# Sliding-window attention and a rational FFN: another form of the division, and work moved off GpSimd while weights are decoded

## The chip, the cores and the metric

The kernel runs on one core of one Trainium2 chip. The metric is the device time of one execution in microseconds (us). Engines are called as in the profile: PE (TensorE), PEld (its weight loads), ACT (ScalarE), DVE (VectorE), POOL (GpSimd), SP (it issues all DMAs).

## The reference

Attention over a window of 64 positions, 8 batches of 576 positions with 8 heads of 64, then a feed-forward layer whose activation is a ratio of two polynomials:

```python
scores = scale * np.matmul(q, k.transpose(0, 1, 3, 2))          # (8, 8, 576, 576)
mask = (rel >= 0) & (rel < 64)
attn = softmax(np.where(mask, scores, -1e9)); x = (attn @ v)    # reshaped to (4608, 512)

h = x @ w_in                                                    # (4608, 2048)
P = a[0] + a[1] * h + a[2] * h**2 + a[3] * h**3
Q = 1.0 + np.abs(b[0]) * np.abs(h) + np.abs(b[1]) * h**2
g = P / (Q + 1e-06)
out = g @ w_out                                                 # (4608, 512)
```

`w_in` and `w_out` come as float64 and reach the core as pairs of 32-bit words.

## The kernel before

The 4608 tokens are cut into 12 chunks of 384 (`CH`). A chunk has 4 attention units (one for each pair of heads) and 16 steps, one for each 128 columns of `w_in`. Matrix products are made in fp32r with split operands: each of x, `w_in`, `w_out` and the gate g is held as a high part (rounded to fp32r) and a low part (what is left), and three products are added up.

- **decode** turns one 128x512 tile of float64 words into fp32: a DMA into `w_st` (two buffers), five integer or max steps on DVE (L113 to L118) through `w_c` (two buffers), a cast to the high part on ACT (L121), and the low part as a difference (L122) on POOL. There are 32 tiles, 16 of each matrix.
- **unit_scores** makes scores on PE, scales and masks them (L188 or L192, two halves), takes the row maximum (L198), six exponentials with sums on ACT (L201), the reciprocal of the sums (L203, L204), and the normalization of `sm` (L205) on POOL. unit_transpose and unit_av follow, and leave x as `xh` (ACT, L228) and `xl` (DVE, L229).
- **ffn1** makes one step: 12 matmuls into `h` (PSUM, two buffers), then the gate. `ah` = |h|; the numerator is built in `num` by ACT (L245) and two DVE products with h (L246, L247); the denominator without its constant in `u` by two POOL operations (L248, L249). The reciprocal of u + QADD is exp(-ln(.)) on ACT (L251, L252) with one Newton step on DVE (L253, L254); L255 finishes the quotient in `num`, ACT casts it to `gh` (L258), and the difference `gl` (L260) is on POOL for the first 20 gates (`GLN`) and on DVE for the rest. `ah`, `u` and `num` have two buffers each, `gh` and `gl` four (`LAG` + 1).
- **ffn2** multiplies a step's gh and gl with `w_out`, 9 matmuls, three steps (`LAG`) behind ffn1, and adds into three PSUM tiles for the chunk, which ACT copies out at the chunk's end (L294).

The first two chunks are interleaved by halves (`phases`), so that only half of the weights is wanted at first. The table `todo` says at which step a tile is loaded or a unit made: four tiles of `w_in` and chunk 0's units come ahead of the first step, the other 28 tiles at steps 0 to 22, chunk 1's units at steps 0 to 4, chunk 2's from step 21. The program is written in this order, and the framework's scheduler then lays down a fixed order of instructions for each engine; each engine works in order and waits on semaphores.

Of the kernel before, what the change touches and what calls it, by code (L numbers as in the profile page):

```python
# [31 lines left out]
def swa_rational_ffn(ctx: ExitStack, tc: tile.TileContext, qT, kT, v, w_in, w_out, a, b, out):  # L32
    nc = tc.nc
    P = 128
# [66 lines left out]
    def decode(src, hi, lo):  # L101

        w = stage.tile([P, 512, 2], U32, name="w_st", bufs=2)
        if len(src.shape) == 3:
# [8 lines left out]
        nc.vector.tensor_scalar(out=c, in0=high, scalar1=0x7FFFFFFF, scalar2=None, op0=ALU.bitwise_and)  # L113
        nc.vector.tensor_scalar(out=cf, in0=cf, scalar1=2.0 ** -15, scalar2=None, op0=ALU.max)

        nc.vector.tensor_scalar(out=c, in0=c, scalar1=3, scalar2=0x3FFFFFF8, op0=ALU.logical_shift_left, op1=ALU.bitwise_and)
        nc.vector.scalar_tensor_tensor(out=c, in0=low, scalar=29, in1=c, op0=ALU.logical_shift_right, op1=ALU.bitwise_or)  # L117
        nc.vector.scalar_tensor_tensor(out=c, in0=high, scalar=0xC0000000, in1=c, op0=ALU.bitwise_and, op1=ALU.bitwise_or)  # L118
# [2 lines left out]
        nc.scalar.copy(out=hi, in_=cf)  # L121
        nc.gpsimd.tensor_tensor(out=lo, in0=cf, in1=hi.bitcast(F32), op=ALU.subtract)  # L122
# [49 lines left out]
    def unit_scores(c, hp):  # L172
        u = live[c, hp]

        ps = ps_a.tile([P, 2, 512], F32, name="ps_s", bufs=1)
# [8 lines left out]
        sm = att.tile([P, 2, PR * P], F32, name="sm")
        m0 = u["m0"]
        for z in range(2):
            if m0 is None:
                nc.vector.scalar_tensor_tensor(out=sm[:, z, :].rearrange("p (r c) -> p r c", c=P),  # L188
                                               in0=ps[:, z, 0:PR * P].rearrange("p (r c) -> p r c", c=P), scalar=SCALE,
                                               in1=mask[:, 1:2, :].broadcast_to([P, PR, P]), op0=ALU.mult, op1=ALU.min)  # L190
            else:
                nc.vector.scalar_tensor_tensor(out=sm[:, z, :], in0=ps[:, z, 0:PR * P], scalar=SCALE,  # L192
                                               in1=mask[:, m0:m0 + PR, :].rearrange("p r c -> p (r c)"),
                                               op0=ALU.mult, op1=ALU.min)
# [3 lines left out]
        nc.vector.tensor_reduce(out=nmx, in_=sm, axis=AX.X, op=ALU.max, negate=True)  # L198
        sums = att.tile([P, NR], F32, name="sums")
        for j in range(NR):  # L200
            nc.scalar.activation(sm[:, j, :], sm[:, j, :], AF.Exp, bias=nmx[:, j:j + 1], accum_out=sums[:, j:j + 1])  # L201
# [2 lines left out]
        nc.vector.reciprocal(out=rs, in_=sums)  # L204
        nc.gpsimd.tensor_tensor(out=sm, in0=sm, in1=rs.unsqueeze(2).broadcast_to([P, NR, P]), op=ALU.mult)  # L205
# [26 lines left out]
    n_gates = [0]  # L232

    def ffn1(c, i):
        h = ps_h.tile([P, CH], F32, name="h")
        n = 0
        for cc in range(NCC):
            for w, x in ((wi_h, xl), (wi_h, xh), (wi_l, xh)):
                nc.tensor.matmul(h, w[:, cc, i * P:(i + 1) * P], x[c, cc], start=n == 0, stop=n == 3 * NCC - 1)  # L239
# [4 lines left out]
        nc.scalar.activation(ah, h, AF.Abs)  # L244
        nc.scalar.activation(num, h, AF.Identity, scale=a_sb[:, 3:4], bias=a_sb[:, 2:3])  # L245
        nc.vector.tensor_tensor(out=num, in0=num, in1=h, op=ALU.mult)  # L246
        nc.vector.scalar_tensor_tensor(out=num, in0=num, scalar=a_sb[:, 1:2], in1=h, op0=ALU.add, op1=ALU.mult)  # L247
# [1 line left out]
        nc.gpsimd.tensor_tensor(out=u, in0=u, in1=ah, op=ALU.mult)  # L249

        nc.scalar.activation(ah, u, AF.Ln, bias=QADD)  # L251
        nc.scalar.activation(ah, ah, AF.Exp, scale=-1.0)  # L252
        nc.vector.scalar_tensor_tensor(out=u, in0=u, scalar=QADD, in1=ah, op0=ALU.add, op1=ALU.mult)  # L253
# [1 line left out]
        nc.vector.scalar_tensor_tensor(out=num, in0=num, scalar=a_sb[:, 0:1], in1=u, op0=ALU.add, op1=ALU.mult)  # L255
        gh = gp.tile([P, CH], F32R, name="gh")
        gl = gp.tile([P, CH], F32R, name="gl")
        nc.scalar.copy(out=gh, in_=num)  # L258
# [1 line left out]
        (nc.gpsimd if n_gates[0] <= GLN else nc.vector).tensor_tensor(out=gl, in0=num, in1=gh.bitcast(F32), op=ALU.subtract)  # L260
# [128 lines left out]
```

## Time and profile before

| | us |
|---|---|
| runs of the kernel before | 1063.88, 1064.74, 1066.21 (median 1064.74) |
| the profiled execution | 1063.77 |
| its span, first to last instruction | 1062.0 |
| busy: PE / DVE / ACT / POOL | 963.7 / 917.7 / 674.3 / 525.0 |
| mean granted TensorE clock | 0.966 |

Times in the profile count from the span's start. In a row of the timeline the first number is the start, the second the duration, then engine, line and operation, the tile written and the tiles read, the shape, how many instructions are merged (x2), and in brackets how long the engine was idle before and what ended that. In a table of windows each engine's busy time stands with its number of instructions, then the granted clock, the DMA engines' share and GB/s. In a list of waits stand the total in us, the number of waits and the longest.

The costliest groups outside PE have, over the whole span: L249 on POOL 204.5 us in 192 instructions, L248 on POOL 164.6 in 192, L260 on DVE 154.0 in 172, L245 on ACT 128.5 in 192, L258 on ACT 96.7 in 192.

### The profile page before, as it was taken

How to read it: one execution, taken by the hardware profiler on the slowest of the kernel's cores; microseconds unless marked ns; L12 is line 12 of the kernel's file. 1: busy time of each engine (PE TensorE's matmuls, PEld its weight loads, DVE VectorE, ACT ScalarE, POOL GpSimd, SP SyncE). 2: the span in 40 equal slices, each digit the busy share in tenths (PEclk: the TensorE clock that was granted, in tenths of full speed). 3: DMA queues.
4: the chain of work that ended last, by engine and by line, in shares of the span. 5: the costliest groups of instructions: out<-in, count | busy, mean ns of one | idle time of the engine just before them, and what ended most of it. 6: DMA issues, size and time to landing. Idle time of an engine off the chain costs nothing.

```text
span 1062.0 us, 18218 instructions
## 1 busy us (share of the span) xinstructions
PE 963.7 (91%) x6624; PEld 846.0 (80%) x6624; DVE 917.7 (86%) x1583; ACT 674.3 (63%) x1702; POOL 525.0 (49%) x511
## 2 busy tenths in 40 slices
PE   2558667899999999999999999999999999999997
PEld 2446555778888888888888888888888888888996
DVE  6999989988888898898888888888888888888885
ACT  3454445467666766766766766766666667667654
POOL 5356658864454445435435535534444444454432
PEclk9778779899999999999999999999999999999999
DMA  5543343102121121110211211210211211200000
GB/s 183 173 152 93 107 130 110 35 1 73 48 66 30 59 58 32 63 61 28 70 45 29 69 48 33 92 31 28 85 29 30 88 30 32 93 16 1 31 2 30
DMA packets 68538, 64.10 MB, mean 60 GB/s; under 512 B 4448, under 2 KB 61792, under 8 KB 68448
## 3 DMA queue, kind: packets, MB, share of 16 engines
q1 hardware_dynamic: 68448, 62.93, 19.0%
q8 instruction: 52, 0.85, 0.3%
q14 instruction: 38, 0.31, 0.1%
HBM read 53.48 MB, written 9.44 MB: 59 GB/s over the span
## 4 chain that ended last, share of the span: by engine, by line
DVE 36%; ACT 20%; POOL 19%; PE 17%; issue 5%; DMA 3%; POOLq 0%; SPq 0%; DVEq 0%; ACTq 0%
PE o L280 8%; ACT sm L201 8%; POOL u L248 7%; PE h L239 7%; DVE u L253 7%; POOL u L249 6%; POOL sm L205 4%; DVE u L254 4%; DVE nmx L198 4%; DVE num L255 2%; ACT ah L251 2%; DVE w_c L117 2%; DVE gl L260 2%; ACT ah L252 2%; DVE w_c L118 2%
## 5 line engine op out<-in xcount | busy, mean ns | idle before, releaser
L239 PE MATMUL h<-xl,wi_h 128*128 128x384 f32 x768 | 269.4, 351 | 30.3 <-DVE num L247 22.3
L248 POOL TENSOR_SCALAR u<-ah,b_sb 128x384 f32<-128x384 f32 x192 | 164.6, 860 | 262.8 <-ACT ah L244 199.6
L239 PE MATMUL h<-xh,wi_h 128*128 128x384 f32 x768 | 264.3, 344 | 0.0
L239 PE MATMUL h<-xh,wi_l 128*128 128x384 f32 x768 | 263.5, 343 | 0.0
L280 PE MATMUL o<-wo_h,gl 128*128 128x512 f32 x576 | 236.8, 411 | 25.4 <-DVE gl L260 14.4
L280 PE MATMUL o<-wo_h,gh 128*128 128x512 f32 x576 | 228.6, 397 | 0.0
L280 PE MATMUL o<-wo_l,gh 128*128 128x512 f32 x576 | 228.0, 396 | 0.0
L249 POOL TENSOR_TENSOR u<-u,ah 128x384 f32<-128x384 f32 x192 | 204.5, 1071 | 9.8
L239 PEld LDWEIGHTS h<-xl,wi_h 128*128 128x128 f32 x768 | 148.2, 193 | 40.1 <-DVE num L247 26.1
L205 POOL TENSOR_TENSOR sm<-sm,rs 128x768 f32<-128x768 f32 x48 | 81.4, 1696 | 195.8 <-DVE rs L204 195.8
L201 ACT ACTIVATE sm<-sm,nmx 128x128 f32<-128x128 f32 x288 | 111.9, 390 | 102.7 <-DVE nmx L198 102.4
L260 DVE TENSOR_TENSOR gl<-num,gh 128x384 fp32r<-128x384 f32 x172 | 154.0, 899 | 13.0 <-ACT gh L258 10.0
L245 ACT ACTIVATE num<-h,a_sb 128x384 f32<-128x384 f32 x192 | 128.5, 670 | 45.7 <-DVE gl L260 35.8
L280 PEld LDWEIGHTS o<-wo_h,gl 128*128 128x128 f32 x576 | 109.6, 190 | 58.9 <-DVE gl L260 19.2
L239 PEld LDWEIGHTS h<-xh,wi_h 128*128 128x128 f32 x768 | 148.5, 193 | 4.7
L253 DVE SCALAR_TENSOR_TENSOR u<-u,ah 128x384 f32<-128x384 f32 x192 | 116.7, 608 | 40.9 <-ACT ah L252 39.2
L251 ACT ACTIVATE ah<-u 128x384 f32<-128x384 f32 x192 | 100.4, 523 | 80.2 <-POOL u L249 79.3
L239 PEld LDWEIGHTS h<-xh,wi_l 128*128 128x128 f32 x768 | 148.3, 193 | 0.0
L280 PEld LDWEIGHTS o<-wo_h,gh 128*128 128x128 f32 x576 | 109.7, 190 | 25.2
L258 ACT CAST gh<-num 128x384 fp32r<-128x384 f32 x192 | 96.7, 508 | 47.5 <-DVE num L255 47.4
L280 PEld LDWEIGHTS o<-wo_l,gh 128*128 128x128 f32 x576 | 109.9, 191 | 18.7
L255 DVE SCALAR_TENSOR_TENSOR num<-num,a_sb,u 128x384 f32<-128x384 f32 x192 | 121.1, 636 | 2.9
(45 smaller groups left out, 1274.1 us busy)
## 6 DMA issues: line engine op xcount, KB each, us to landing
out<-ob SPq DMA_DIRECT2D x33, 256.0 KB, 2.0
w_st<-w_in SPq DMA_DIRECT2D x16, 512.0 KB, 3.7
w_st<-w_out SPq DMA_DIRECT2D x16, 512.0 KB, 3.6
q<-qT SPq DMA_DIRECT2D x32, 192.0 KB, 3.4
vt<-v SPq DMA_DIRECT2D x16, 384.0 KB, 3.4
vt<-v SPq DMA_DIRECT2D x16, 320.0 KB, 3.3
kt<-kT SPq DMA_DIRECT2D x16, 224.0 KB, 3.5
kt<-kT SPq DMA_DIRECT2D x16, 192.0 KB, 3.5
```

The costliest lines, as they stand in the source:

```text
L201: nc.scalar.activation(sm[:, j, :], sm[:, j, :], AF.Exp, bias=nmx[:, j:j + 1], accum_out=sums[:, j:j + 1])
L205: nc.gpsimd.tensor_tensor(out=sm, in0=sm, in1=rs.unsqueeze(2).broadcast_to([P, NR, P]), op=ALU.mult)
L239: nc.tensor.matmul(h, w[:, cc, i * P:(i + 1) * P], x[c, cc], start=n == 0, stop=n == 3 * NCC - 1)
L245: nc.scalar.activation(num, h, AF.Identity, scale=a_sb[:, 3:4], bias=a_sb[:, 2:3])
L248: nc.gpsimd.tensor_scalar(out=u, in0=ah, scalar1=b_sb[:, 1:2], scalar2=b_sb[:, 0:1], op0=ALU.mult, op1=ALU.add)
L249: nc.gpsimd.tensor_tensor(out=u, in0=u, in1=ah, op=ALU.mult)
L251: nc.scalar.activation(ah, u, AF.Ln, bias=QADD)
L253: nc.vector.scalar_tensor_tensor(out=u, in0=u, scalar=QADD, in1=ah, op0=ALU.add, op1=ALU.mult)
L255: nc.vector.scalar_tensor_tensor(out=num, in0=num, scalar=a_sb[:, 0:1], in1=u, op0=ALU.add, op1=ALU.mult)
L258: nc.scalar.copy(out=gh, in_=num)
L260: (nc.gpsimd if n_gates[0] <= GLN else nc.vector).tensor_tensor(out=gl, in0=num, in1=gh.bitcast(F32), op=ALU.subtract)
L280: nc.tensor.matmul(acc[c][t], g[:, ts], w[:, i, :], start=first and n == 0, stop=last and n == 2)
```

## The change

Four things change.

1. In decode, the absolute value of the high word is made by ACT (a floating-point Abs of the word) and no longer by DVE, and the low part's difference goes from POOL to DVE.
2. The normalization of `sm` is made by DVE for the units of chunks 0 and 1 (8 of 48).
3. In the gate, the step b1 * ah + b0 goes from POOL to ACT, for all steps. The product u * ah is made by DVE for the first 28 gates (`DEC`) and stays on POOL for the others.
4. The division: with r = exp(-ln(Q)), gh is written at once as (num + a0) * r, rounded to fp32r; u becomes Q * gh; num becomes (num + a0) - u, the remainder; gl = num * r, the low part. So the Newton step and ACT's cast are gone, DVE still has four steps after Exp, and `ah` (which holds r) is read until the last of them.

```diff
-GLN = 20
+DEC = 28
...
-        nc.vector.tensor_scalar(out=c, in0=high, scalar1=0x7FFFFFFF, scalar2=None, op0=ALU.bitwise_and)
+        nc.scalar.activation(cf, w.bitcast(F32)[:, :, 1], AF.Abs)
...
-        nc.gpsimd.tensor_tensor(out=lo, in0=cf, in1=hi.bitcast(F32), op=ALU.subtract)
+        nc.vector.tensor_tensor(out=lo, in0=cf, in1=hi.bitcast(F32), op=ALU.subtract)
...
-        nc.gpsimd.tensor_tensor(out=sm, in0=sm, in1=rs.unsqueeze(2).broadcast_to([P, NR, P]), op=ALU.mult)
+        (nc.vector if c < 2 else nc.gpsimd).tensor_tensor(out=sm, in0=sm, in1=rs.unsqueeze(2).broadcast_to([P, NR, P]), op=ALU.mult)
...
+        gh = gp.tile([P, CH], F32R, name="gh")
+        gl = gp.tile([P, CH], F32R, name="gl")
         nc.scalar.activation(ah, h, AF.Abs)
         nc.scalar.activation(num, h, AF.Identity, scale=a_sb[:, 3:4], bias=a_sb[:, 2:3])
+        nc.scalar.activation(u, ah, AF.Identity, scale=b_sb[:, 1:2], bias=b_sb[:, 0:1])
         nc.vector.tensor_tensor(out=num, in0=num, in1=h, op=ALU.mult)
         nc.vector.scalar_tensor_tensor(out=num, in0=num, scalar=a_sb[:, 1:2], in1=h, op0=ALU.add, op1=ALU.mult)
-        nc.gpsimd.tensor_scalar(out=u, in0=ah, scalar1=b_sb[:, 1:2], scalar2=b_sb[:, 0:1], op0=ALU.mult, op1=ALU.add)
-        nc.gpsimd.tensor_tensor(out=u, in0=u, in1=ah, op=ALU.mult)
+        n_gates[0] += 1
+        (nc.vector if n_gates[0] <= DEC else nc.gpsimd).tensor_tensor(out=u, in0=u, in1=ah, op=ALU.mult)
 
         nc.scalar.activation(ah, u, AF.Ln, bias=QADD)
         nc.scalar.activation(ah, ah, AF.Exp, scale=-1.0)
-        nc.vector.scalar_tensor_tensor(out=u, in0=u, scalar=QADD, in1=ah, op0=ALU.add, op1=ALU.mult)
-        nc.vector.scalar_tensor_tensor(out=u, in0=u, scalar=2.0, in1=ah, op0=ALU.subtract, op1=ALU.mult, reverse0=True)
-        nc.vector.scalar_tensor_tensor(out=num, in0=num, scalar=a_sb[:, 0:1], in1=u, op0=ALU.add, op1=ALU.mult)
-        nc.scalar.copy(out=gh, in_=num)
-        n_gates[0] += 1
-        (nc.gpsimd if n_gates[0] <= GLN else nc.vector).tensor_tensor(out=gl, in0=num, in1=gh.bitcast(F32), op=ALU.subtract)
+        nc.vector.scalar_tensor_tensor(out=gh, in0=num, scalar=a_sb[:, 0:1], in1=ah, op0=ALU.add, op1=ALU.mult)
+        nc.vector.scalar_tensor_tensor(out=u, in0=u, scalar=QADD, in1=gh.bitcast(F32), op0=ALU.add, op1=ALU.mult)
+        nc.vector.scalar_tensor_tensor(out=num, in0=num, scalar=a_sb[:, 0:1], in1=u, op0=ALU.add, op1=ALU.subtract)
+        nc.vector.tensor_tensor(out=gl, in0=num, in1=ah, op=ALU.mult)
```

The new kernel's lines of the gate are L246 to L248 (ACT: Abs, num, u), L249 and L250 (DVE: the products with h), L252 (u * ah), L255 and L256 (Ln, Exp), L257 to L260 (gh, u, num, gl).

The scheduler lays the engines' orders anew. DVE in the ramp, around the second pair of gates, before (`w_c` and `w_st` are the tile in decoding, L229 is an attention unit's):

```order
L113 TENSOR_SCALAR w_c<-w_st 128x512
L114 TENSOR_SCALAR w_c<-w_c 128x512
L229 TENSOR_TENSOR xl_651<-ps_x,xh_650 128x384
L116 TENSOR_SCALAR w_c<-w_c 128x512
L117 SCALAR_TENSOR_TENSOR w_c<-w_st,w_c 128x512
L253 SCALAR_TENSOR_TENSOR u<-u,ah 128x384
L118 SCALAR_TENSOR_TENSOR w_c<-w_st,w_c 128x512
L254 SCALAR_TENSOR_TENSOR u<-u,ah 128x384
L246 TENSOR_TENSOR num<-num,h 128x384
L247 SCALAR_TENSOR_TENSOR num<-num,a_sb,h 128x384
```

The same place of DVE's new order:

```order
L116 TENSOR_SCALAR w_c<-w_c 128x512
L249 TENSOR_TENSOR num<-num,h 128x384
L117 SCALAR_TENSOR_TENSOR w_c<-w_st,w_c 128x512
L252 TENSOR_TENSOR u<-u,ah 128x384
L250 SCALAR_TENSOR_TENSOR num<-num,a_sb,h 128x384
L117 SCALAR_TENSOR_TENSOR w_c<-w_st,w_c 128x512
L252 TENSOR_TENSOR u<-u,ah 128x384
L250 SCALAR_TENSOR_TENSOR num<-num,a_sb,h 128x384
L118 SCALAR_TENSOR_TENSOR w_c<-w_st,w_c 128x512 x2
L257 SCALAR_TENSOR_TENSOR gh<-num,a_sb,ah 128x384
```

Two tiles and two gates now advance in turn, with the products u * ah (L252) between them; L122, the low part, stands a few rows further on.

ACT in the long stage, one pair of steps with an attention unit, before. The number behind a tile's name tells the two steps of the pair apart:

```order
L258 CAST gh_5072<-num_5060 128x384
L244 ACTIVATE ah_5173<-h_5160 128x384
L258 CAST gh_5112<-num_5100 128x384
L245 ACTIVATE num_5175<-h_5160,a_sb_90 128x384
L244 ACTIVATE ah_5239<-h_5226 128x384
L245 ACTIVATE num_5241<-h_5226,a_sb_90 128x384
L251 ACTIVATE ah_5173<-u_5174 128x384
L228 CAST xh3_4992<-ps_x_4979 128x384
L252 ACTIVATE ah_5173<-ah_5173 128x384
L251 ACTIVATE ah_5239<-u_5240 128x384
L252 ACTIVATE ah_5239<-ah_5239 128x384
L201 ACTIVATE sm_5135,sums_5140<-sm_5135,nmx_5138 128x128 x6
```

The same place of ACT's new order:

```order
L246 ACTIVATE ah_5095<-h_5082 128x384
L247 ACTIVATE num_5097<-h_5082,a_sb_90 128x384
L248 ACTIVATE u_5096<-ah_5095,b_sb_92 128x384
L246 ACTIVATE ah_5160<-h_5147 128x384
L247 ACTIVATE num_5162<-h_5147,a_sb_90 128x384
L248 ACTIVATE u_5161<-ah_5160,b_sb_92 128x384
L255 ACTIVATE ah_5095<-u_5096 128x384
L228 CAST xh3_4917<-ps_x_4904 128x384
L256 ACTIVATE ah_5095<-ah_5095 128x384
L255 ACTIVATE ah_5160<-u_5161 128x384
L256 ACTIVATE ah_5160<-ah_5160 128x384
L201 ACTIVATE sm_5057,sums_5062<-sm_5057,nmx_5060 128x128 x6
```

Before, the gh casts of a pair stand behind the six exponentials and among the next pair's first steps; now nothing of a pair is left on ACT behind its last Exp, and each step has three operations at its start.

DVE at the same place, before, the end of a pair with a unit:

```order
L198 TENSOR_REDUCE nmx_5138<-sm_5135 128x6
L255 SCALAR_TENSOR_TENSOR num_5175<-num_5175,a_sb_90,u_5174 128x384
L254 SCALAR_TENSOR_TENSOR u_5240<-u_5240,ah_5239 128x384
L255 SCALAR_TENSOR_TENSOR num_5241<-num_5241,a_sb_90,u_5240 128x384
L203 TENSOR_SCALAR sums_5140<-sums_5140 128x6
L204 RECIPROCAL rs_5147<-sums_5140 128x6
L260 TENSOR_TENSOR gl_5188<-num_5175,gh_5187 128x384
L260 TENSOR_TENSOR gl_5254<-num_5241,gh_5253 128x384
```

And now:

```order
L257 SCALAR_TENSOR_TENSOR gh_4664<-num_4663,a_sb_90,ah_4661 128x384
L257 SCALAR_TENSOR_TENSOR gh_4729<-num_4728,a_sb_90,ah_4726 128x384
L198 TENSOR_REDUCE nmx_4626<-sm_4623 128x6
L258 SCALAR_TENSOR_TENSOR u_4662<-u_4662,gh_4664 128x384
L258 SCALAR_TENSOR_TENSOR u_4727<-u_4727,gh_4729 128x384
L259 SCALAR_TENSOR_TENSOR num_4663<-num_4663,a_sb_90,u_4662 128x384
L259 SCALAR_TENSOR_TENSOR num_4728<-num_4728,a_sb_90,u_4727 128x384
L260 TENSOR_TENSOR gl_4665<-num_4663,ah_4661 128x384
L260 TENSOR_TENSOR gl_4730<-num_4728,ah_4726 128x384
L203 TENSOR_SCALAR sums_4628<-sums_4628 128x6
L204 RECIPROCAL rs_4635<-sums_4628 128x6
```

The two gl stood behind the unit's sums (L203, L204), which need the exponentials; now they stand ahead of them.

More of the change, by code (lines that the diff above doesn't have):

```diff
@@ L243, in ffn1 @@
         num = tmp.tile([P, CH], F32, name="num")
+        gh = gp.tile([P, CH], F32R, name="gh")
+        gl = gp.tile([P, CH], F32R, name="gl")
         nc.scalar.activation(ah, h, AF.Abs)
         nc.scalar.activation(num, h, AF.Identity, scale=a_sb[:, 3:4], bias=a_sb[:, 2:3])
+        nc.scalar.activation(u, ah, AF.Identity, scale=b_sb[:, 1:2], bias=b_sb[:, 0:1])
         nc.vector.tensor_tensor(out=num, in0=num, in1=h, op=ALU.mult)
         nc.vector.scalar_tensor_tensor(out=num, in0=num, scalar=a_sb[:, 1:2], in1=h, op0=ALU.add, op1=ALU.mult)
-        nc.gpsimd.tensor_scalar(out=u, in0=ah, scalar1=b_sb[:, 1:2], scalar2=b_sb[:, 0:1], op0=ALU.mult, op1=ALU.add)
-        nc.gpsimd.tensor_tensor(out=u, in0=u, in1=ah, op=ALU.mult)
+        n_gates[0] += 1
+        (nc.vector if n_gates[0] <= DEC else nc.gpsimd).tensor_tensor(out=u, in0=u, in1=ah, op=ALU.mult)
         nc.scalar.activation(ah, u, AF.Ln, bias=QADD)
         nc.scalar.activation(ah, ah, AF.Exp, scale=-1.0)
-        nc.vector.scalar_tensor_tensor(out=u, in0=u, scalar=QADD, in1=ah, op0=ALU.add, op1=ALU.mult)
-        nc.vector.scalar_tensor_tensor(out=u, in0=u, scalar=2.0, in1=ah, op0=ALU.subtract, op1=ALU.mult, reverse0=True)
[L255 to L258, printed above, removed]
-        n_gates[0] += 1
-        (nc.gpsimd if n_gates[0] <= GLN else nc.vector).tensor_tensor(out=gl, in0=num, in1=gh.bitcast(F32), op=ALU.subtract)
+        nc.vector.scalar_tensor_tensor(out=gh, in0=num, scalar=a_sb[:, 0:1], in1=ah, op0=ALU.add, op1=ALU.mult)
+        nc.vector.scalar_tensor_tensor(out=u, in0=u, scalar=QADD, in1=gh.bitcast(F32), op0=ALU.add, op1=ALU.mult)
+        nc.vector.scalar_tensor_tensor(out=num, in0=num, scalar=a_sb[:, 0:1], in1=u, op0=ALU.add, op1=ALU.subtract)
+        nc.vector.tensor_tensor(out=gl, in0=num, in1=ah, op=ALU.mult)
         gs[c, i] = gh, gl
```

## Prediction

> **What bounds the kernel now.** I read the page first, then the busy time by stage, then who ended the waits of PE in the long stage.
>
> ```profile
> PE   2558667899999999999999999999999999999997
> DVE  6999989988888898898888888888888888888885
> POOL 5356658864454445435435535534444444454432
> ```
>
> Each digit is 26.5 us. The kernel has two stages. In the first eight slices DVE is full and PE is not; in the rest PE is full. The busy times say it in us:
>
> ```profile
> 0.00:207.00 207.00, 128.82 (x880) 107.00 (x881) 189.06 (x299) 96.04 (x257) 129.53 (x118) 0.83 0.40 124
> 266.00:1040.00 774.00, 762.03 (x5329) 677.65 (x5330) 665.62 (x1182) 530.01 (x1334) 359.46 (x358) 1.00 0.15 45
> ```
>
> The columns are PE, PEld, DVE, ACT, POOL, then the granted clock. Up to 207 us, about where the last weight tile is decoded, DVE works 189 of 207 us and PE waits. From 266 to 1040 us PE works 762 of 774 us at full clock. Its 12 us of idle time there have one cause:
>
> ```profile
> PE o L280 <- DVE gl L260: 12.2, 10, 1.6
> ```
>
> Ten waits, one for each 16-step chunk, for the low part gl of a gate. So there are two places to win: the ramp, paced by DVE, and these ten waits. Everything else after 266 us is matmul work that the change does not touch.
>
> **Why DVE takes so long in the ramp.** Two stretches of DVE and what POOL did in the second:
>
> ```profile
> 9.00 0.43 DVE L116 TENSOR_SCALAR w_c<-w_c 128x512 uint32<-128x512 uint32 x1
> 9.34 1.02 DVE L192 SCALAR_TENSOR_TENSOR sm<-ps_s,mask 128x384 f32<-128x384 f32 x2
> 10.27 0.68 DVE L117 SCALAR_TENSOR_TENSOR w_c<-w_st,w_c 128x512 uint32<-128x512 uint32 x1
> 10.87 0.94 DVE L198 TENSOR_REDUCE nmx<-sm 128x6 f32<-128x768 f32 x1
> 11.73 0.68 DVE L118 SCALAR_TENSOR_TENSOR w_c<-w_st,w_c 128x512 uint32<-128x512 uint32 x1
> 12.33 0.42 DVE L113 TENSOR_SCALAR w_c<-w_st 128x512 uint32<-128x512 uint32 x1
> ...
> 17.40 1.57 DVE L114 TENSOR_SCALAR w_c<-w_c 128x512 f32<-128x512 f32 x1
> 19.47 1.64 DVE L117 SCALAR_TENSOR_TENSOR w_c<-w_st,w_c 128x512 uint32<-128x512 uint32 x1
> ```
>
> ```profile
> 17.14 1.55 POOL L205 TENSOR_TENSOR sm<-sm,rs 128x768 f32<-128x768 f32 x1 [0.73 <-DVE rs L204]
> 19.18 1.38 POOL L122 TENSOR_TENSOR wi_l<-w_c,wi_h 128x512 fp32r<-128x512 f32 x1 [0.49 <-ACT wi_h L121]
> ```
>
> The columns are start and duration in us. The L114 at 17.40 lies under the POOL multiply of 17.14 to 18.69 and takes 1.57 us where its kind takes 0.42; the L117 at 19.47 lies under the POOL subtraction and takes 1.64 instead of 0.68. DVE's decode steps stop while POOL works in SBUF. The price of an operation without that is its distance to the next start: 0.34 us for a one-input 128x512 step (9.00 to 9.34), 0.60 for a two-input one (10.27 to 10.87), 0.93 for both mask steps of a unit, 0.86 for the reduction. The gate's own prices:
>
> ```profile
> 87.18 0.55 DVE L246 TENSOR_TENSOR num<-num,h 128x384 f32<-128x384 f32 x1
> 87.64 0.61 DVE L255 SCALAR_TENSOR_TENSOR num<-num,a_sb,u 128x384 f32<-128x384 f32 x1
> 88.17 0.42 DVE L114 TENSOR_SCALAR w_c<-w_c 128x512 f32<-128x512 f32 x1
> 88.51 0.61 DVE L247 SCALAR_TENSOR_TENSOR num<-num,a_sb,h 128x384 f32<-128x384 f32 x1
> 89.03 1.14 DVE L116 TENSOR_SCALAR w_c<-w_c 128x512 uint32<-128x512 uint32 x1
> 90.09 0.55 DVE L253 SCALAR_TENSOR_TENSOR u<-u,ah 128x384 f32<-128x384 f32 x1
> 90.56 0.41 DVE L113 TENSOR_SCALAR w_c<-w_st 128x512 uint32<-128x512 uint32 x1
> ```
>
> 0.46 for a product, 0.53 with a coefficient from a_sb, 0.47 for L253.
>
> **The ramp after the change.** I count DVE's list of the new order up to the last decoded tile: 32 decodes, 11 attention units, 20 gate fronts (two products with h), 20 products u*ah, and 18 to 20 of each of the four closing steps.
> - Decode: two one-input steps (L113 has gone to ACT) and three two-input ones (the subtraction has come from POOL; 0.60, priced as the equally large L117): 2 x 0.34 + 3 x 0.60 = 2.48 us, x32 = 79.4.
> - Units: 0.93 + 0.86 + about 0.7 for the small ones and xl = 2.5, x11 = 27; the normalization that eight of them bring from POOL, 768 elements like the reduction, 0.87, x8 = 7.
> - Gates: 0.46 + 0.53 + 0.47 (the new product) = 1.46, x20 = 29; closing steps 0.53 + 0.47 + 0.53 + 0.47 = 2.0, some x18.5 = 37.
>
> Together 179 us. Before, the list up to the last tile costs 135 us by the same prices (32 x 2.22 for decodes, 10 units, 16 gates), and DVE was busy 189: some 54 us are contention. So the change brings DVE about 36 us of POOL's work and takes nearly all the contention away.
>
> To this come the start, 8.1 us until the first tile lands (first DVE step, 8.08) and 0.6 for ACT's new Abs ahead of it (priced as the casts of a tile), and the time DVE waits within the ramp: 207 - 189 - 8 = 10 us before. Now decoding goes from ACT to DVE to ACT to DVE, so I take more, 17. Bounds: 4 (the order interleaves two tiles and two gates, so little is left open) and 30 (three times today's). The list ends at 179 + 9 + 17 = 205, between 192 and 218. The kernel before is as far, 18 closed gates, here:
>
> ```profile
> 0.00:221.30 221.30, 0.00 (x0) 23.18 (x18) 0.84 0.38 118
> ...
> 219.93 1.31 POOL L260 TENSOR_TENSOR gl<-num,gh 128x384 fp32r<-128x384 f32 x1
> ```
>
> The first is L260 alone: 18 by 221.3. From there PE is dense in both, so the ramp's gain is 221 - 205 = 16, bounds 3 and 29. I take 15, for the units of the third chunk, whose multiply POOL still does at the end of the ramp. ACT has 96 us in 207 and gains 32 Abs of about 0.6 and one exchange of a gh cast for an affine step: some 23 more, no bound. PE's 129 us are covered too.
>
> **A rule against it.** The spacing of DVE's rows carries the sum: 0.46 between starts where the duration is 0.55. The Trainium skill, VectorE: DVE Perf Modes, section "The DRAIN you can't avoid", says that after each DVE operation the next does not start until the pipe is empty. By that every operation costs its duration; with some 365 operations and 0.08 us each the list would be 29 us longer. The rows above disagree with it in that form (87.18 + 0.55 ends behind the start at 87.64).
>
> **The long stage after the change.** gl no longer waits for ACT's gh cast; ACT has an affine step instead (L248), and POOL only the product. But all temporaries have two buffers, and ah now lives until gl, so a pair of steps cannot begin before the pair ahead has closed. That loop must be shorter than PE's work. Prices and PE's pace:
>
> ```profile
> 546.53 0.49 ACT L244 ACTIVATE ah<-h 128x384 f32<-128x384 f32 x1 [0.69 <-PE h L239]
> 546.92 0.67 ACT L245 ACTIVATE num<-h,a_sb 128x384 f32<-128x384 f32 x1
> 547.48 0.51 ACT L258 CAST gh<-num 128x384 fp32r<-128x384 f32 x1
> ...
> 551.21 0.52 ACT L251 ACTIVATE ah<-u 128x384 f32<-128x384 f32 x1
> 551.75 0.53 ACT L252 ACTIVATE ah<-ah 128x384 f32<-128x384 f32 x1
> 555.04 0.40 ACT L201 ACTIVATE sm<-sm,nmx 128x128 f32<-128x128 f32 x1 [2.76 <-DVE nmx L198]
> ...
> 555.44 0.39 ACT L201 ACTIVATE sm<-sm,nmx 128x128 f32<-128x128 f32 x1
> ```
>
> ```profile
> 547.98 1.01 POOL L249 TENSOR_TENSOR u<-u,ah 128x384 f32<-128x384 f32 x1
> ...
> 558.07 1.72 POOL L205 TENSOR_TENSOR sm<-sm,rs 128x768 f32<-128x768 f32 x1 [7.04 <-DVE rs L204]
> ```
>
> ```profile
> 539.31 4.41 PE o L280 x18
> ...
> 617.82 4.41 PE o L280 x18
> ```
>
> A chunk takes 78.5 us (539.31 to 617.82); without its wait of 1.2 PE needs 77.3, or 19.3 for four steps and a unit. The loop, walked by the new order from the first Abs, with 0.1 for a hand-over (an estimate from the rows' gaps):
> - Pair without a unit: ACT needs 2 x (0.39 + 0.56 + 0.56) = 3.0 for Abs, num and the affine step (unknown; between L252's 0.53 and L245's 0.67, I take the latter, since both read two coefficients). POOL's second product ends at 4.2, the second Ln and Exp at 5.3, the second gh starts at 5.4; then num, u and gl of the first step: its gl ends at 7.5, and the next Abs starts at 7.6.
> - Pair with a unit: on DVE from 3.9 on xl 0.47, masks 0.93, gh twice 1.06, reduction 0.86, u twice 0.94, num twice 1.06, gl 0.55: 9.8. ACT's six exponentials of 0.39 run from 7.3 to 9.7 beside it. POOL's normalization (1.72) then delays the next product by 0.9 and that pair by 0.5.
>
> 7.6 + 9.8 + 0.5 = 17.9 against 19.3: PE stays the bound with 1.4 us to spare, and gl comes without the six exponentials in front of its cast. So I take all 12 us of waits as gone; bounds 0 and 12.
>
> **Sum.** Span 1062.0 - 15 - 12 = 1035.0; the execution's own time is 1063.77, so 1.8 more: 1036.8. That execution lies 1 us under the median of 1064.74. I forecast 1037.
>
> **Rivals.**
> 1. The loop of pairs becomes the bound. For it speaks that ACT already waits for gl:
> ```profile
> ACT num L245 <- DVE gl L260: 35.8, 67, 1.3
> ```
> Against it, the walk. It decides from 20.0 us per four steps on: the stage has 774 / 19.6 = 39.5 groups, each now 19.6 with the waits, and 0.4 x 39.5 eats the ramp's 15. At 20.5 it would be 1064 - 15 + 0.9 x 39.5 = 1084, slower. Chance 0.10.
> 2. The ramp does not shorten: ACT, which works in order, waits for tiles and lets DVE wait. DVE would need 32 us of waits in place of 17, beyond my upper bound. 1064 - 12 = 1052. Chance 0.14.
> 3. The ten waits stay, because gl is late for another reason (the three copies of o at a chunk's end, on ACT): 1064 - 15 = 1049. Chance 0.14.
> 4. Both 2 and 3; within 0.2% of before, 1064. Chance 0.05.
> 5. DVE's operations cost their durations: the ramp 29 - 15 = 14 longer, the waits gone: 1066, at the edge of slower. Chance 0.03. This is the skill's rule above.
>
> The forecast itself, 1024 (bounds 29 and 12) to 1049, has 0.52; still more gain 0.02.
>
> **Range and chances.** 0.2% (2 us) is about what a measurement can tell. Faster: 0.52 + 0.02 + 0.14 + 0.14 = 0.82. Same 0.05. Slower 0.10 + 0.03 = 0.13. The range 1021 to 1058 holds the forecast's cases and rivals 2 and 3, and leaves out rivals 1, 4 and 5.
>
> **What would show it.** Decode steps on DVE at 0.42 and 0.68 throughout; the last tile decoded before 207 us; DVE busy about 180 us up to there; no PE wait for gl between 266 and 1040, PE busy above 770 of 774 there. Wrong, if ACT's first Abs of a pair waits for gl while PE waits for h, if DVE's idle time in the ramp is over 30 us, or if DVE's two-input steps stay at 1 us and more.

## The result and the profile after

| | before | after |
|---|---|---|
| median (lowest to highest), us | 1065.47 (1063.88 to 1066.47) | 1023.91 (1023.07 to 1025.14) |
| span of the profiled execution | 1062.0 | 1023.3 |
| 18th low part gl done at | 221.2 | 191.7 |
| last tile decoded at | 209.6 | 200.6 |
| from the 18th gl to the end | 840.8 | 831.6 |

The ratio is 0.9612 (0.9595 to 0.9629). The span is 38.7 us shorter: 29.5 up to the 18th closed gate and 9.2 behind it.

The page after, busy tenths in 40 slices, now 25.6 us each:

```profile
PE   2677876899999999999999999999999999999997
DVE  5999999998878878878878878878888888888785
POOL 2000010002322322322322322322322322322221
```

POOL is nearly empty in the first nine slices. DVE is as full there as before, so it is still the busiest engine of the ramp, but it comes through sooner. PE is full from the ninth slice on.

The windows of the kernel after (PE, PEld, DVE, ACT, POOL, clock, DMA share, GB/s):

```profile
0.00:191.70 191.70, 127.86 (x932) 105.41 (x933) 175.92 (x351) 120.27 (x307) 14.10 (x30) 0.90 0.45 136
...
192.00:207.00 15.00, 14.23 (x63) 12.08 (x62) 14.33 (x28) 11.21 (x23) 0.00 (x0) 0.89 0.01 1
...
0.00:200.70 200.70, 136.86 (x969) 113.26 (x970) 184.38 (x367) 127.04 (x319) 14.10 (x30) 0.90 0.43 130
...
266.00:1000.00 734.00, 734.00 (x5162) 655.80 (x5161) 596.18 (x1140) 542.46 (x1293) 207.58 (x190) 1.00 0.15 46
```

The same milestone before:

```profile
0.00:221.20 221.20, 141.55 (x951) 117.71 (x951) 200.50 (x317) 104.47 (x282) 138.77 (x126) 0.84 0.38 118
```

To the 18th gl DVE now issues 351 instructions in 175.9 us; before it was 317 in 200.5. So it does 34 more in 24.6 us less. By the prediction's prices this list is some 145 us before and 173 after; the busy time lies 56 us above the one and 3 us above the other.

In the long stage PE works 734.00 of 734.00 us, and no wait of PE is left between 266 and 1000 us. (Behind 1000 us there is one of 2.0 us for gl; before there was one of 2.2.)

The 18th gl is not quite the same point in both kernels: in the kernel after, PE has 19 matmuls fewer behind it there (932 and 951), and the low parts of two tiles are still to be made. In the 15 us behind it PE makes 63 matmuls, so 19 are 4.5 us of work. This makes the ramp worth 29.5 - 4.5 = 25 us and the rest 9.2 + 4.5 = 13.7. A count of PE's starts in the traces says the same: the 1300th matmul starts at 249.6 us, before at 274.5. Of the 13.7 us, 12.2 are waits for gl that are gone; no run separates the other 1.5.

The decode steps on DVE, by lines, before (up to 207 us) and after (up to 192 us); the second number after the bar is the mean in ns:

```profile
L118 DVE SCALAR_TENSOR_TENSOR w_c<-w_st,w_c 128x512 uint32<-128x512 uint32 x32 | 33.0, 1035 | 0.1
L117 DVE SCALAR_TENSOR_TENSOR w_c<-w_st,w_c 128x512 uint32<-128x512 uint32 x32 | 30.6, 959 | 0.3
L114 DVE TENSOR_SCALAR w_c<-w_c 128x512 f32<-128x512 f32 x32 | 20.8, 648 | 0.3
L116 DVE TENSOR_SCALAR w_c<-w_c 128x512 uint32<-128x512 uint32 x32 | 19.9, 621 | 0.3
```

```profile
L118 DVE SCALAR_TENSOR_TENSOR w_c<-w_st,w_c 128x512 uint32<-128x512 uint32 x31 | 21.1, 684 | 0.1
L117 DVE SCALAR_TENSOR_TENSOR w_c<-w_st,w_c 128x512 uint32<-128x512 uint32 x31 | 21.1, 684 | 0.1
L114 DVE TENSOR_SCALAR w_c<-w_c 128x512 f32<-128x512 f32 x31 | 14.5, 468 | 12.8 <-ACT w_c L113 12.8
L116 DVE TENSOR_SCALAR w_c<-w_c 128x512 uint32<-128x512 uint32 x31 | 13.0, 419 | 0.1
```

The same four steps are 28 to 34% shorter. What DVE waited for in the first 192 us of the kernel after (us in total, times, longest):

```profile
DVE w_c L114 <- ACT w_c L113: 12.8, 8, 8.4
DVE sums L203 <- ACT sm L201: 1.1, 3, 0.6
DVE sm L188 <- PE ps_s L182: 0.7, 1, 0.7
DVE wi_l L122 <- ACT wi_h L121: 0.3, 1, 0.3
DVE xl L229 <- ACT xh L228: 0.2, 1, 0.2
```

The longest, 8.4, is the start of the program, until the first tile has landed and ACT has made its Abs. Without it 6.7 us are left.

ACT in the long stage (266 to 1000 us), its waits for h and gl, after and before:

```profile
ACT ah L246 <- PE h L239: 75.9, 83, 3.8
...
ACT ah L246 <- DVE gl L260: 2.5, 2, 2.1
```

```profile
ACT num L245 <- DVE gl L260: 34.9, 63, 1.3
...
ACT ah L244 <- PE h L239: 12.8, 19, 0.9
```

Before, the head of a pair waited mostly for the low part of the pair ahead. Now it waits for PE's h, 83 times, and for gl twice: there it is PE that is waited for. The chain that ended last says the same, before and then after:

```profile
DVE 36%; ACT 20%; POOL 19%; PE 17%; issue 5%; DMA 3%; POOLq 0%; SPq 0%; DVEq 0%; ACTq 0%
```

```profile
PE 81%; DVE 11%; ACT 3%; DMA 3%; issue 1%; POOL 0%; SPq 0%; POOLq 0%; ACTq 0%; DVEq 0%
```

### The profile page after: what moved, and what is told of

The parts are those of the page before. It is cut to its first block, busy times and chain, and to the rows that moved or that the text cites. A ratio compares the mean times of both kernels' runs of the same rounds, so it can differ in the third digit from the quotient of the medians.

```text
span 1023.3 us, 18244 instructions
## 1 busy us (share of the span) xinstructions
PE 953.1 (93%) x6624; PEld 840.4 (82%) x6624; DVE 850.3 (83%) x1639; ACT 725.8 (71%) x1734; POOL 233.7 (23%) x231
## 4 chain that ended last, share of the span: by engine, by line
PE 81%; DVE 11%; ACT 3%; DMA 3%; issue 1%; POOL 0%; SPq 0%; POOLq 0%; ACTq 0%; DVEq 0%
PE o L280 37%; PE h L239 35%; PE ps_x L223 3%; PE ps_s L182 3%; PE ps_s L212 3%; DMA w_st<-w_in 1%; DVE w_c L117 1%; DMA w_st<-w_out 1%; ACT sm L201 1%; DVE w_c L118 1%; DVE num L259 1%; DVE gh L257 1%; DVE u L258 1%; DVE num L249 1%; DVE num L250 1%
## 5 line engine op out<-in xcount | busy, mean ns | idle before, releaser
L239 PE MATMUL h<-xl,wi_h 128*128 128x384 f32 x768 | 264.9, 345 | 14.8 <-DVE num L250 8.6
L239 PE MATMUL h<-xh,wi_l 128*128 128x384 f32 x768 | 259.7, 338 | 0.0
L280 PE MATMUL o<-wo_h,gl 128*128 128x512 f32 x576 | 238.1, 413 | 22.3 <-DVE gl L260 22.3
L252 POOL TENSOR_TENSOR u<-u,ah 128x384 f32<-128x384 f32 x164 | 166.7, 1017 | 317.3 <-ACT u L248 278.7
L249 DVE TENSOR_TENSOR num<-num,h 128x384 f32<-128x384 f32 x192 | 106.1, 553 | 108.9 <-ACT num L247 108.7
L246 ACT ACTIVATE ah<-h 128x384 f32<-128x384 f32 x192 | 94.3, 491 | 108.1 <-PE h L239 83.3
L205 POOL TENSOR_TENSOR sm<-sm,rs 128x768 f32<-128x768 f32 x40 | 61.7, 1541 | 457.9 <-DVE rs L204 352.3
L280 PEld LDWEIGHTS o<-wo_h,gl 128*128 128x128 f32 x576 | 111.3, 193 | 51.3 <-DVE gl L260 24.6
L248 ACT ACTIVATE u<-ah,b_sb 128x384 f32<-128x384 f32 x192 | 135.4, 706 | 0.0
L257 DVE SCALAR_TENSOR_TENSOR gh<-num,a_sb,ah 128x384 fp32r<-128x384 f32 x192 | 114.8, 615 | 17.6 <-ACT ah L256 16.9
L250 DVE SCALAR_TENSOR_TENSOR num<-num,a_sb,h 128x384 f32<-128x384 f32 x192 | 117.9, 614 | 5.9
L259 DVE SCALAR_TENSOR_TENSOR num<-num,a_sb,u 128x384 f32<-128x384 f32 x192 | 115.8, 620 | 0.8
```

Of the source, the lines that this page charges most:

```text
L205: (nc.vector if c < 2 else nc.gpsimd).tensor_tensor(out=sm, in0=sm, in1=rs.unsqueeze(2).broadcast_to([P, NR, P]), op=ALU.mult)
L248: nc.scalar.activation(u, ah, AF.Identity, scale=b_sb[:, 1:2], bias=b_sb[:, 0:1])
L252: (nc.vector if n_gates[0] <= DEC else nc.gpsimd).tensor_tensor(out=u, in0=u, in1=ah, op=ALU.mult)
L257: nc.vector.scalar_tensor_tensor(out=gh, in0=num, scalar=a_sb[:, 0:1], in1=ah, op0=ALU.add, op1=ALU.mult)
L280: nc.tensor.matmul(acc[c][t], g[:, ts], w[:, i, :], start=first and n == 0, stop=last and n == 2)
```

## Experiments

The theory: the ramp's gain is contention taken from DVE's operations, the long stage's gain is the new gate. The rivals are in each expectation. The last four columns are of the profiled execution, in us; "it" is the 18th gl. The kernel before had medians of 1065.5 to 1066.0 beside these runs.

| run | median us | ratio to before (95%) | 18th gl at | from there on | DVE busy to it | POOL busy to it |
|---|---|---|---|---|---|---|
| after | 1023.91 | 0.9612 (0.9595 to 0.9629) | 191.7 | 831.6 | 175.9 | 14.1 |
| e1_gate_only | 1041.11 | 0.9765 (0.9749 to 0.9781) | 215.5 | 824.5 | 198.9 | 92.6 |
| e2_offload_only | 1048.35 | 0.9826 (0.9810 to 0.9841) | 200.2 | 846.2 | 182.9 | 12.1 |
| e3_pool_reads | 1087.46 | 1.0202 (1.0187 to 1.0217) | 248.1 | 837.0 | 237.5 | 137.0 |
| e4_pool_writes | 1039.91 | 0.9745 (0.9728 to 0.9763) | 202.0 | 836.2 | 188.0 | 139.4 |
| e5_lo_pool | 1036.26 | 0.9722 (0.9708 to 0.9737) | 206.2 | 828.6 | 189.8 | 59.9 |
| e6_dec0 | 1023.24 | 0.9601 (0.9585 to 0.9617) | 195.3 | 825.8 | 178.6 | 35.4 |
| e7_sm_pool | 1030.20 | 0.9664 (0.9649 to 0.9678) | 199.4 | 826.9 | 180.8 | 28.1 |
| e8_abs_dve | 1036.74 | 0.9732 (0.9716 to 0.9749) | 205.4 | 828.6 | 188.9 | 16.0 |
| e9_affine_act | 1058.21 | 0.9930 (0.9916 to 0.9945) | 212.3 | 845.1 | 195.3 | 115.4 |
| e10_skip_low | 1014.23 | 0.9523 (0.9507 to 0.9539) | 184.0 | 827.3 | 161.8 | 12.1 |
| e11_sm_act | 1025.01 | 0.9623 (0.9608 to 0.9637) | 195.9 | 829.2 | 175.9 | 12.4 |
| e12_sm_act_skip_low | 1016.68 | 0.9541 (0.9526 to 0.9555) | 187.4 | 828.3 | 157.8 | 11.9 |

### The two halves of the change

**e1_gate_only** is the kernel after with decode, the normalizations and the product u * ah (on POOL) as before:

```diff
-DEC = 28
+DEC = 0
-        nc.scalar.activation(cf, w.bitcast(F32)[:, :, 1], AF.Abs)
+        nc.vector.tensor_scalar(out=c, in0=high, scalar1=0x7FFFFFFF, scalar2=None, op0=ALU.bitwise_and)
-        nc.vector.tensor_tensor(out=lo, in0=cf, in1=hi.bitcast(F32), op=ALU.subtract)
+        nc.gpsimd.tensor_tensor(out=lo, in0=cf, in1=hi.bitcast(F32), op=ALU.subtract)
-        (nc.vector if c < 2 else nc.gpsimd).tensor_tensor(out=sm, in0=sm, in1=rs.unsqueeze(2).broadcast_to([P, NR, P]), op=ALU.mult)
+        nc.gpsimd.tensor_tensor(out=sm, in0=sm, in1=rs.unsqueeze(2).broadcast_to([P, NR, P]), op=ALU.mult)
```

> The new gate alone: the division by remainder and the affine step on ACT for all steps, while the decode (its Abs on DVE, its low part on POOL), the normalization of sm and the product u*ah stay where they were before. Theory A (POOL's reads of SBUF stall DVE in the ramp, and the gl wait of the long stage is one of order on ACT): the ten waits of PE for gl go (12 us); in the ramp POOL loses the affine step (22 us) and the 20 gl (21 us) of its 130 us, so a third of the 54 us of contention, 18, and DVE gains 16 x 0.47 = 7.5 us: 11 less. Span 1062 - 23 = 1039, time near 1041. Theory B (the ramp is paced by hops between engines, and POOL's company costs DVE nothing): the gate has one hop fewer, the ramp stays within 3 us, time near 1052.

**e2_offload_only** is the complement: the old division and cast, and POOL empty in the ramp.

```diff
-        nc.scalar.activation(u, ah, AF.Identity, scale=b_sb[:, 1:2], bias=b_sb[:, 0:1])
-        (nc.vector if n_gates[0] <= DEC else nc.gpsimd).tensor_tensor(out=u, in0=u, in1=ah, op=ALU.mult)
+        eng = nc.vector if n_gates[0] <= DEC else nc.gpsimd
+        eng.tensor_scalar(out=u, in0=ah, scalar1=b_sb[:, 1:2], scalar2=b_sb[:, 0:1], op0=ALU.mult, op1=ALU.add)
+        eng.tensor_tensor(out=u, in0=u, in1=ah, op=ALU.mult)
...
+        nc.scalar.copy(out=gh, in_=num)
+        nc.vector.tensor_tensor(out=gl, in0=num, in1=gh.bitcast(F32), op=ALU.subtract)
```

> The old division (Newton step, gh cast on ACT, gl as a difference, always on DVE), with everything else of the change: Abs on ACT, the low part and the first 8 normalizations on DVE, and both steps of u on DVE for the first 28 gates, on POOL after. Theory A: DVE's list in the ramp is that of the changed kernel plus 20 one-input steps of about 0.3 us, 6 us, so the ramp is some 20 to 24 us shorter than before; the ten gl waits stay, 12 us. Time near 1042. Theory B: DVE has some 45 us more work in the ramp and no relief, time 1065 or more.

PE's waits between 266 and 1000 us, all that are listed, in e1_gate_only and then in e2_offload_only:

```profile
PE o L280 <- DVE gl L260: 0.5, 1, 0.5
```

```profile
PE o L281 <- DVE gl L261: 12.2, 9, 1.5
```

The new gate alone takes the ten waits away but for 0.5 us, and the empty POOL alone leaves them as they were. The ramp goes mostly the other way: the 18th gl comes 6 us sooner than before with the gate alone (215.5) and 21 us sooner with the offload alone (200.2). So the waits go with the gate, most of the ramp's gain goes with the offload, and the spans add up: 22.0 + 15.6 = 37.6 of 38.7.

e1_gate_only came out at its expected time, but partly by luck: 5.7 us were won up to the 18th gl where 11 were expected, and 16.3 behind it where 12 were. e2_offload_only came 6 us above its expectation: behind its 18th gl it needs 846.2 us, 5.4 more than the kernel before. Its last tile is decoded only at 211.5, and DVE has one step more than in the kernel after for each of the first 28 gates; that this is the cause was not tested.

### Is it contention, and with what?

**e3_pool_reads** gives POOL three multiplies for each tile, on a scratch tile for which nothing waits. DVE, ACT and PE have the work of the kernel after.

```diff
+    dm = const.tile([P, 760], F32, name="dm")
+    nc.gpsimd.memset(dm, 0.0)
...
+        for _ in range(3):
+            nc.gpsimd.tensor_tensor(out=dm[:, 0:512], in0=dm[:, 0:512], in1=dm[:, 0:512], op=ALU.mult)
```

> The changed kernel with 96 multiplies of a 128x512 scratch tile by itself on POOL, from the start on, which nothing waits for (some 125 us of POOL reading and writing SBUF, as much as POOL worked in the ramp before). Theory A: DVE's two-input and one-input SBUF steps take up to twice their time while these run, as before: the ramp is 40 to 55 us longer, time 1064 to 1080. Theory B: nothing depends on them, time 1024 to 1027.

**e4_pool_writes** gives POOL about as much work, but work that only writes:

```diff
+        for _ in range(5):
+            nc.gpsimd.memset(dm, 0.0)
```

> The same with 160 memsets of a 128x760 scratch tile on POOL instead, which only write (some 120 us). If it is POOL's reads that stall DVE, two-input steps are free and at most the 64 one-input decode steps slow down: 1024 to 1034. If any access of POOL to SBUF does it, as with the multiplies: 1064 to 1080. Theory B: 1024 to 1027.

The decode steps and POOL's work by lines. First e3_pool_reads to 137 us, then e4_pool_writes to 110 us (L119 and L120 there are the two-input steps L117 and L118 of the kernel after, L116 and L118 the one-input steps L114 and L116; L196 is the mask step, which has one input in PSUM):

```profile
L119 DVE SCALAR_TENSOR_TENSOR w_c<-w_st,w_c 128x512 uint32<-128x512 uint32 x15 | 17.6, 1179 | 0.1
L116 DVE TENSOR_SCALAR w_c<-w_c 128x512 f32<-128x512 f32 x15 | 14.2, 944 | 8.7 <-ACT w_c L115 8.7
L120 DVE SCALAR_TENSOR_TENSOR w_c<-w_st,w_c 128x512 uint32<-128x512 uint32 x15 | 13.7, 920 | 0.1
L118 DVE TENSOR_SCALAR w_c<-w_c 128x512 uint32<-128x512 uint32 x15 | 13.3, 886 | 0.1
...
L196 DVE SCALAR_TENSOR_TENSOR sm<-ps_s,mask 128x384 f32<-128x384 f32 x14 | 7.1, 543 | 0.0
...
L125 POOL TENSOR_TENSOR dm<-dm 128x512 f32<-128x512 f32 x83 | 105.8, 1275 | 6.4
```

```profile
L118 DVE TENSOR_SCALAR w_c<-w_c 128x512 uint32<-128x512 uint32 x17 | 12.1, 711 | 0.1
L116 DVE TENSOR_SCALAR w_c<-w_c 128x512 f32<-128x512 f32 x17 | 11.7, 690 | 10.4 <-ACT w_c L115 10.3
L120 DVE SCALAR_TENSOR_TENSOR w_c<-w_st,w_c 128x512 uint32<-128x512 uint32 x17 | 11.6, 684 | 0.1
L119 DVE SCALAR_TENSOR_TENSOR w_c<-w_st,w_c 128x512 uint32<-128x512 uint32 x17 | 11.5, 681 | 0.1
...
L125 POOL MEMSET dm<- 128x760 f32 x121 | 94.3, 780 | 6.9
```

With POOL reading, the two-input steps take 0.92 and 1.18 in place of 0.68, the one-input ones about 0.9 in place of 0.42 to 0.47, and more than the whole gain is gone: 1087 us, 2% slower than before and 7 us above what the expectation allowed. The mask step, which reads only one of its two inputs from SBUF, stays at 0.54 (0.55 in the kernel after). DVE's list is that of the kernel after, so the loss is POOL's company. PE's granted clock up to the 18th gl fell with it, from 0.90 to 0.82, though only POOL was given more to do: the 0.84 of the kernel before can be a sign of its slow ramp, and need not be a cause. With POOL writing, the two-input steps stay at 0.68 as in the empty kernel, and only the one-input steps grow, from 0.42 to 0.47 up to 0.69 to 0.71. The Trainium skill, SBUF — State Buffer, section "Who interferes with whom", says this: DVE operations with two SBUF inputs contend with a GpSimd instruction that reads SBUF and not with one that only writes, and the two-port modes of one-input steps contend with either. Both runs agree with it, by these rows. The price is 61.6 us of DVE busy time (237.5 - 175.9) for 123 us more of POOL's multiplies, half a us for each, and 12 us for 125 us more of writes.

e4_pool_writes missed its expectation by 6 us. Its 18th gl comes 10.3 us later than in the kernel after, as DVE's 12 us ask. Another 4.6 lie behind it, where POOL's added work is over; 3 of them are PE's pace in the long stage, whose cause is open (last section).

### Which of the moves pay

**e5_lo_pool** (the low part back on POOL), **e6_dec0** (u * ah on POOL from the first gate), **e7_sm_pool** (all normalizations on POOL) and **e8_abs_dve** (the absolute value back on DVE) each undo one move:

```diff
e5:
-        nc.vector.tensor_tensor(out=lo, in0=cf, in1=hi.bitcast(F32), op=ALU.subtract)
+        nc.gpsimd.tensor_tensor(out=lo, in0=cf, in1=hi.bitcast(F32), op=ALU.subtract)
e6:
-DEC = 28
+DEC = 0
e7:
-        (nc.vector if c < 2 else nc.gpsimd).tensor_tensor(out=sm, in0=sm, in1=rs.unsqueeze(2).broadcast_to([P, NR, P]), op=ALU.mult)
+        nc.gpsimd.tensor_tensor(out=sm, in0=sm, in1=rs.unsqueeze(2).broadcast_to([P, NR, P]), op=ALU.mult)
e8:
-        nc.scalar.activation(cf, w.bitcast(F32)[:, :, 1], AF.Abs)
+        nc.vector.tensor_scalar(out=c, in0=high, scalar1=0x7FFFFFFF, scalar2=None, op0=ALU.bitwise_and)
```

> The changed kernel with the decode's low part back on POOL. Two accounts of what a move off POOL brings in the ramp. Account L (a linear price): 1 us of POOL reading SBUF costs DVE 0.42 us (54 us for 129.5 before; 62 for 126 in the run with added multiplies). 32 differences of 1.4 us on POOL cost DVE 19 us and spare it 32 x 0.60 = 19: no difference, 1021 to 1027. Account S (the whole gain of the ramp comes from emptying POOL, so each move gains its share): slower by 8 us or more, from 1032.

> The changed kernel with u*ah on POOL from the first gate. Account L: 18 products of 1.05 us up to the 18th gate cost DVE 8 us and spare it 18 x 0.47 = 8.5: no difference, 1021 to 1027. Account S: slower by 4 us or more, from 1028. Both leave out the hops DVE to POOL and back, which can add a few us.

> The changed kernel with all normalizations on POOL. Account L: eight of 1.5 us cost DVE 5 us and spare it 8 x 0.87 = 7: 1021 to 1025. Account S: slower by 3 us or more.

> The changed kernel with the high word's absolute value on DVE again. DVE paces the ramp, so 32 x 0.34 = 11 us are added to its list and hardly anything is freed: 1032 to 1036 by both accounts. If ACT's part of the ramp, or the hop from ACT to DVE at a tile's start, is the pace, the time stays or falls: up to 1024.

The windows to the 18th gl of e5, e6, e7 and e8, in this order:

```profile
0.00:206.30 206.30, 137.75 (x952) 113.65 (x952) 189.92 (x331) 125.99 (x315) 59.88 (x62) 0.88 0.41 127
```

```profile
0.00:195.40 195.40, 133.23 (x951) 111.33 (x952) 178.69 (x342) 125.09 (x315) 35.43 (x49) 0.90 0.44 134
```

```profile
0.00:199.50 199.50, 131.50 (x935) 109.35 (x936) 180.87 (x350) 124.10 (x312) 28.08 (x38) 0.85 0.43 131
```

```profile
0.00:205.50 205.50, 134.63 (x936) 111.60 (x937) 188.97 (x388) 105.62 (x279) 15.97 (x30) 0.84 0.42 127
```

e5 is 12.4 us slower than the kernel after: DVE does 20 instructions fewer and is busy 14.0 us longer. Counted by line against the kernel after, DVE's list up to there lacks 30 subtractions and has two more decode steps of each kind and one more of each gate step: by the prediction's prices 13 us less. So 27 us are contention, from 46 us more of POOL. The same count gives 9 us from 14 us of POOL in e7 (6.3 us slower) and 7 us from 21 in e6, where what DVE loses to contention is about what it saves by not making the products: no difference. From 0.3 to 0.6 us are lost for each us of POOL, so there is no one price. The account that reckoned with a linear one (L) missed e5 by at least 9 us and e7 by at least 5; the other (S) held in these two and missed e6 by 5, where L held.

e8 is 12.8 us slower, 0.7 above its range, with 13.0 us more DVE work and POOL nearly as empty as in the kernel after: here the added DVE work comes out one to one. Of the four moves, three pay; the u * ah move does not. Undone one at a time they cost 31 us in all, undone together (e1_gate_only) 17.2, so these are not shares that add up.

### What the gh cast and the affine step did apart

**e9_affine_act** is the kernel before with the affine step of the denominator on ACT and nothing else:

```diff
+        nc.scalar.activation(u, ah, AF.Identity, scale=b_sb[:, 1:2], bias=b_sb[:, 0:1])
-        nc.gpsimd.tensor_scalar(out=u, in0=ah, scalar1=b_sb[:, 1:2], scalar2=b_sb[:, 0:1], op0=ALU.mult, op1=ALU.add)
```

> The kernel before with one move alone: the step b1*ah + b0 goes from POOL to ACT, the old division stays. It tells why PE's ten waits for gl went. If it is the order (gl stands behind ACT's cast gh, and that behind the unit's six exponentials), the ten waits stay, 10 us or more between 266 and 1000 us; the ramp gains what 22 us less of POOL cost DVE, 9 us: 1055 to 1058. If it is POOL's company, which made gl take 1.2 us, the waits shrink below 5 us with POOL's load: 1044 to 1050.

PE's waits between 266 and 1000 us:

```profile
PE o L280 <- DVE gl L260: 4.4, 6, 0.9
PE h L239 <- DVE num L248: 0.9, 1, 0.9
PE o L280 <- DVE ob L292: 0.2, 1, 0.2
```

By its time the run lies with "order", just above its 1055 to 1058. Its waits fell from 12.2 to 5.5, 4.4 of them for gl, which "order" did not allow and "company" did; but gl itself takes hardly less than before (0.92 us and 0.95, from 320 to 960 us), which was the reason that "company" gave. So neither holds as it was put. Two thirds of the waits for gl went with POOL's affine step; with the new division as well (e1_gate_only) 0.5 is left. The time shows little of it: from its 18th gl on the run needs 845.1 us, the kernel before 840.8.

Why moving the affine step helps gl, which stands behind ACT's cast and not behind POOL, no run settles. The traces allow one way. ACT's Ln waits for POOL's product, and it waits less with the affine step on ACT (before, then e9, 266 to 1000 us):

```profile
ACT ah L251 <- POOL u L249: 68.1, 100, 1.5
```

```profile
ACT ah L251 <- POOL u L249: 31.1, 43, 1.1
```

A gate that comes sooner to its Ln also comes sooner to its cast and its gl. This is argued and not shown, and the new division without the move of the affine step was not run.

### What paces the ramp now

**e10_skip_low** leaves out one DVE step of decode (the weights are then cut off), **e11_sm_act** makes the first eight normalizations on ACT, and **e12_sm_act_skip_low** does both:

```diff
e10:
-        nc.vector.scalar_tensor_tensor(out=c, in0=low, scalar=29, in1=c, op0=ALU.logical_shift_right, op1=ALU.bitwise_or)
e11:
-        (nc.vector if c < 2 else nc.gpsimd).tensor_tensor(out=sm, in0=sm, in1=rs.unsqueeze(2).broadcast_to([P, NR, P]), op=ALU.mult)
+        if c < 2:
+            for j in range(NR):
+                nc.scalar.activation(sm[:, j, :], sm[:, j, :], AF.Identity, scale=rs[:, j:j + 1])
+        else:
+            nc.gpsimd.tensor_tensor(out=sm, in0=sm, in1=rs.unsqueeze(2).broadcast_to([P, NR, P]), op=ALU.mult)
```

> The changed kernel without L117, which puts the upper three bits of a weight's low word into the lowest three bits of the fp32 mantissa: the weights are cut off there. It takes 32 two-input steps of 0.60 us, 19 us, from DVE's list in the ramp. If DVE still paces the ramp: 15 to 19 us less, 1005 to 1009. If the ramp is now paced by tiles' landing, ACT or PE: 1017 or more.

> The changed kernel with the eight normalizations on ACT as six scaled copies each, in place of one DVE product. DVE's list loses 8 x 0.87 = 7 us, ACT (120 of 192 us busy in the ramp) gains 48 copies of 0.39 us, 18. If DVE's list is the pace: 1017 to 1020. If ACT's order begins to hold DVE up: 1024 or more.

> Both of these, with the weights cut off in the same way. If DVE's list is the pace, 26 us less: 998 to 1002. If ACT (then 138 us of a ramp of some 165) takes over, no better than without L117 alone, 1006 or more.

The windows to the 18th gl of e10, e11 and e12:

```profile
0.00:184.10 184.10, 126.28 (x932) 104.89 (x933) 161.82 (x326) 122.83 (x312) 12.11 (x30) 0.91 0.45 142
```

```profile
0.00:196.00 196.00, 133.93 (x940) 110.46 (x941) 175.92 (x352) 138.49 (x363) 12.44 (x30) 0.89 0.43 133
```

```profile
0.00:187.50 187.50, 127.45 (x938) 106.20 (x939) 157.79 (x320) 136.76 (x362) 11.88 (x30) 0.88 0.45 139
```

e10 takes 14 us of busy time from DVE; the 18th gl comes 7.7 earlier and the end 9.7, so that the time lies between the two ranges that were expected. DVE's idle time (window less busy) grows from 15.8 to 22.3. e11 gains nothing, though ACT has only 138 of 196 us; e12 is slower than e10, with 29.7 us idle on DVE. Both lie where ACT's order was expected to hold DVE up. So DVE no longer paces the ramp alone: work added to it costs its whole time (e8), work taken from it comes back by half to two thirds, and work moved from it to ACT not at all. What ACT waits for there is in the kernel after, first 192 us:

```profile
ACT w_c L113 <- DMA w_st<-w_out: 15.2, 9, 3.5
ACT w_c L113 <- DMA w_st<-w_in: 13.9, 5, 5.7
ACT ah L246 <- DVE gl L260: 9.2, 5, 5.2
ACT wo_h L121 <- DVE w_c L118: 8.0, 4, 3.0
```

ACT stands 29 us, the start included, behind tiles that have not landed. A tile can be loaded only when one of the two `w_st` buffers is free, and the last to read a buffer is DVE (L118), so part of this can still be DVE's pace. Whether a third `w_st` buffer would help was not tried. None of the versions with the whole weights beats the kernel after; e6_dec0 equals it.

## Why the prediction was right, and where its sizes were off

The forecast was 1037, the time 1024. Both gains came, at the places and by the mechanisms that were named; the ramp's was sized too small, 15 us where it is 25. The time lies at the very edge of the forecast's own case (1024 to 1049).

- **Long stage: right.** Forecast: all 12 us of waits gone, PE at once the bound. Measured: no wait from 266 to 1000 us, where 12.2 us stood. The slack that the walk gave, 1.4 us for four steps, shows in ACT's waits for h: 75.9 us in 734 / 19.2 = 38 groups, 2.0 each. The affine step, taken as 0.67, has 0.705 in the kernel after:

```profile
L248 ACT ACTIVATE u<-ah,b_sb 128x384 f32<-128x384 f32 x134 | 94.5, 705 | 0.0
```

- **Contention: right.** 54 us of it were read from busy time less list; after, 3 are left, and e3_pool_reads put the contention back and lost the gain.
- **DVE's list: right within 5 us.** 179 us to the last tile were forecast; DVE was busy 184.4 there (the row to 200.7 us). Rival 5 is out: by durations the list alone would have been 29 us longer. The sentence that the prediction took from the Trainium skill (VectorE: DVE Perf Modes, "The DRAIN you can't avoid") is not all that the section says: it adds that a next operation which is not held starts earlier. The prediction's rows agree with that addition (0.46 us from start to start where the duration is 0.55).
- **DVE's waiting in the ramp: the mis-sized term.** The step "now decoding goes from ACT to DVE to ACT to DVE, so I take more, 17" was wrong. Up to the last tile, at 200.6 us, DVE is idle 16.3 us; the start takes 8.4 of them, and 7.9 are left, much nearer to the lower bound of 4. The new order lets two tiles and two gates advance in turn, which the prediction itself had seen; that this is why the hand-overs cost so little was not tested. So the ramp ended some 4 us before the forecast 205: 9 from this term and 0.6 from the start, less 5 for the list.
- **The milestone.** The prediction measured the ramp before by the 18th gl (221.2) and after by the last tile. These are not the same point: in the kernel after the 18th gl comes 9 us ahead of the last tile, and at 200.6 PE has made 969 matmuls, the number that the kernel before reaches at 225.3. This hid another 4 us of the gain, so that 16 us forecast (taken as 15) became 25. That the errors of the list and of the waiting had opposite signs is luck.
- The rivals: 1 (the loop of pairs) is out by ACT's waits, 2 by the ramp's 25 us, 3 and 4 by the empty list of PE's waits.
